# Attention feeding two mixture layers on one core: reciprocals of the row sums alone, value products in one step, the w3 @ w_out products last in the plan

## The chip, the cores and the metric

The kernel runs on one core of a Trainium2 chip. The metric is the time of one execution on the device in microseconds; lower is better. The kernel before was run three times.

## What is computed

The reference chains three blocks. Cut to what matters:

```python
# attention: batch 2, 8 heads, 576 positions, head size 64
q_rot, k_rot = rotate(q), rotate(k)
scores = q_rot @ k_rot^T / sqrt(64);  scores -= rowmax
attn = exp(scores);  attn /= rowsum(attn) + 1e-9
x = (attn @ v) laid out as 1152 x 512
# first mixture: d_model 512, d_ff 1024
h = ((x @ w1) * (x @ w2)) @ w3
x = h @ w_out
# second mixture: 8 experts, gate P balanced in 8 rounds of row and column sums
out = sum_e P[:, e] * (relu(x @ w1[e]) @ w2[e])
```

The kernel multiplies w3 @ w_out once (512 columns), so that the first mixture needs one product with the result in place of two.

## The kernel before, in words

**Attention.** A pair is two heads of one batch; there are 8 pairs (`NP`). Per pair, keys and queries are loaded, rotated (`rope_mul`, `rope_add`, `rope_hi`, `rope_lo`) and spread over partitions by DMAs from the SP queue (`spread_k`, `spread_q`). The 576 queries of each head make four tiles of 128 and one mixed tile that holds the last 64 of both heads. For every tile TensorE (PE) makes the scores (lines 340 and 363), VectorE (DVE) the negated row maximum (`row_max`, line 370), ScalarE (ACT) the exponentials with their sums in `sm` (line 374), PE transposes the exponentials (lines 388 and 391), and ACT or DVE moves them to `et` (`moved`, line 407).

Two groups of tiles (`TILES`) then have a normaliser each. `norm_sums` (line 411, ACT) adds 1e-9 to the 4 or 5 sums per partition, `norm_rows` (line 418, DVE) takes the reciprocal of the sums broadcast to 64 columns each, so of 128x256 or 128x320 elements, into `rb`; `norm_columns` (lines 424 and 427, PE) transposes that, `norm_moved` (line 432, ACT) copies it to `r`. `values` (line 440, PE) is five steps per group, two matmuls each (one per head, on the two halves of PSUM tile `x`), and `x_scale` (line 448, DVE) multiplies by `r`. `x_hi` and `x_lo` (lines 459 and 463) split the result in two parts for the fp32r products that follow. `psX` holds one PSUM tile, so the next group's first value product waits for `x_scale` of this one.

**w3 @ w_out beside it.** The weights come as 64-bit words. `wide_parts` joins their halves: ACT line 183, DVE lines 188, 191 and 196, ACT line 201 (high part), and line 204 (low part) on POOL or DVE. Eight units of w_out and sixteen of w3 are converted; there are two slots for w3. A unit of w3 gives four steps of `w34_product` (lines 231 to 233), three matmuls of 512 columns each, and frees its slot at the fourth. Two units make one of the eight row blocks, which `w34_hi` and `w34_lo` (lines 238 and 243) take out of PSUM; six blocks use `psW`, which has one tile, the seventh uses `psT`, and the eighth (`NEARLY`) comes after the plan.

**What orders it.** `Plan` (line 52) is a greedy list scheduler that runs when the kernel is built. Every step has engine costs, a rank, needs and buffers; at each moment the ready step of least rank goes out, and the resulting static order is each engine's program. The planned cost of `norm_rows` is that of a plain DVE operation of its size. Ranks of attention run with the pair's number (18 for each pair), those of `w34_product` are 87 + 4u + j for unit u and step j. Until the first `w34_product` the planned gaps on PE are filled with small matmuls (line 615).

**After the plan.** `branch` (lines 145 to 147) computes x @ w1 and x @ w2, whose weights `w12_unit` converts in the same way; the eight steps of the eighth block stand just ahead of it. `merge`, then `hidden` and `project` over the experts follow.

Of the kernel before, what the change touches and what calls it, by code (L numbers as in the profile page):

```python
# [18 lines left out]
P = 128  # L19
B, H, S, D = 2, 8, 576, 64  # L20
# [7 lines left out]
MID = NBLK // 2  # L28
SPAD = 640
NQ = NBLK // 2 + 1  # L30
MIX = NQ - 1
SF = 2 * P
HS = S // 2
G0, G1 = 256, S - 256
HD = P // 2
TILES = (0, 1), (2, 3, 4)
CN = 320, 256
# [83 lines left out]
def attention_two_moes(ctx: ExitStack, tc: tile.TileContext, rope, qk, v, mw12, mw3t, mwo, wg, ew1, ew2, out):  # L121
# [7 lines left out]
    pe, act, dve, pool, sp = nc.tensor, nc.scalar, nc.vector, nc.gpsimd, nc.sync  # L129
# [12 lines left out]
    def three(ps, terms):  # L142
# [15 lines left out]
    psS, psT, psX, psW = (  # L158
        aps.enter_context(tc.tile_pool(name=n, bufs=k, space=PSUM)) for n, k in (("psS", 2), ("psT", 2), ("psX", 1), ("psW", 1))
    )  # L160
# [63 lines left out]
    def w34_product(u, j, ps_pool, name):  # L224

        i, k = u // 2, u % 2 * 4 + j
        if k == 0:
            w34[i] = ps_pool.tile([P, DM], F32, name=name)
        (h, l, _), (oh, ol, _) = w3[u], wo[k]
        c = slice(j * P, (j + 1) * P)  # L230
        pe.matmul(w34[i], h[:, c], oh, start=(k == 0), stop=False)
        pe.matmul(w34[i], h[:, c], ol, start=False, stop=False)
        pe.matmul(w34[i], l[:, c], oh, start=False, stop=(k == KF - 1))
# [16 lines left out]
    V = [att_p.tile([P, NBLK + 1, D], F32, name=f"v{i}") for i in range(2)]  # L250
# [7 lines left out]
    raw, K, st = {}, {}, {}  # L258
# [37 lines left out]
    def spread_q(n, j, x):  # L296
# [5 lines left out]
        else:  # L302
            sp.dma_start(dst[:, : MIX * P], src[:, : MIX * P])
            sp.dma_start(dst[:, MIX * P + HD :], src[:, MIX * P :])

# [7 lines left out]
    def half(j):  # L313
        return slice(j * D, (j + 1) * D)
# [97 lines left out]

    def norm_rows(n, g):

        k = 4 + g
        sm = st["sm", n, g][:, :k]
        st["rb", n, g] = rb = att_p.tile([P, 5, D], F32, name="rb", bufs=2)
        dve.reciprocal(rb[:, :k], sm.unsqueeze(2).to_broadcast([P, k, D]))

    def norm_columns(n, g):  # L420
        rb = st["rb", n, g]
# [9 lines left out]
        ng = (G0, G1)[g]  # L431
        act.copy(r[:, :ng], st["rt", n, g].rearrange("p i q -> p (i q)")[:, :ng])

    def values(n, g, t):

        ng = (G0, G1)[g]
        if t == 0:
            st["x", n, g] = psX.tile([P, DM], F32, name="x")
        for j in range(2):
            pe.matmul(  # L440
                st["x", n, g][half(j), :ng], V[n % 2][:, 2 * t + j], st["et", n, g][:, 2 * t + j * (t < MID)],
                start=(t == 0), stop=(t == MID),
            )

    def x_scale(n, g):
        ng = (G0, G1)[g]
# [20 lines left out]
    def step(f, args, costs, rank, needs=(), takes=(), frees=(), **kw):  # L467

        many = f in (rope_mul, rope_add, rope_lo, moved, x_lo)
        plan.step((f, *args), costs, rank, lambda e: f(*args, ENG[e]) if many else f(*args), needs, takes, frees, **kw)  # L470


    act_ps, act_sb = (lambda n: 0.12 + n / 1450), (lambda n: 0.1 + n / 1190)
    on_dve, on_pool, moving = (lambda n: 0.09 + n / 945), (lambda n: 0.1 + n / 440), (lambda n: n / 250e3)
# [6 lines left out]
    for n in range(NP):  # L481
        t = n * NQ * TILE
        step(load_v, (n,), {"sp": moving(4 * P * (NBLK + 1) * D)}, t - 40.0, takes=[("v", n)])
        ready = []
        for w in (1, 0):
            pieces = (every,) if n else halves if w else (slice(0, SF), slice(SF, S))
            for c in pieces:
                a, m = (n, w, c), c.stop - c.start
                r = t - 30.0 if n else -50.0 if c.start == 0 or w else -40.0
# [8 lines left out]
                fr = [("raw", (n, w))] if n == 0 and c is pieces[-1] else []  # L498
# [6 lines left out]
            for j, x in ((j, x) for j in range(2) for x in range(2)):  # L505
# [4 lines left out]
                else:  # L510
                    needs = [((rope_hi, rope_lo)[x], n, 0, every)]
# [3 lines left out]
        for i in range(NQ):  # L515
            g, k, _ = group(i)
            r = t + i * TILE
            for j in range(2 - (i == MIX)):
# [3 lines left out]
                fr = [("kk", n), ("sq", n)] if n and i == MIX else []  # L522
                needs = ready[0] + (ready[1] if n or i * P >= SF else ready[1][:1]) + before
# [3 lines left out]
                else:  # L527
                    made = mixed_scores, n
                    if n == 0:
                        for q in range(2):  # L530
                            step(mix_first, (q,), {"act": 0.2}, r, ready[1])
                        needs = needs + [(mix_first, 0), (mix_first, 1)]
# [3 lines left out]
                fr = [("psS", (n, i, j))] + [("nm", (n, i))] * (j or i == MIX)  # L536
                step(exponentials, (n, i, j), {"act": 0.73}, r, [(row_max, n, i, j)], frees=fr)
            r += TILE
            parts = 3 - (i == MIX)
            for p in range(parts):  # L540
                needs = [(exponentials, n, i, min(p, 1) * (i < MIX))] + ([(transposes, n, i, p - 1)] if p else [(transposes, n, i - 1, 0)] if k else [])
                tk = [("psT", (n, i, p))] + ([(f"et{g}", n)] if k == p == 0 else [])
                step(transposes, (n, i, p), {"pe": 0.33}, r, needs, tk, [("e", (n, i))] if p == parts - 1 else [])
                m = 3 * (P if i < MIX else P - HD * p)
                step(moved, (n, i, p), {"act": act_ps(m), "dve": on_dve(m)}, r, [(transposes, n, i, p)], frees=[("psT", (n, i, p))])
        for g, tiles in enumerate(TILES):
            a, ng = (n, g), (G0, G1)[g]
            r = t + (tiles[-1] + 2.0) * TILE
            needs = [(exponentials, n, i, j) for i in tiles for j in range(2 - (i == MIX))]
            step(norm_sums, a, {"act": 0.2}, r, needs)  # L550
            step(norm_rows, a, {"dve": on_dve((4 + g) * D)}, r, [(norm_sums, *a)], [("rb", a)], [("sm", a)])
            step(norm_columns, a, {"pe": (0.24, 0.4)[g]}, r, [(norm_rows, *a)], [("psT", (*a, "r"))], [("rb", a)])
            step(norm_moved, a, {"act": act_ps(ng)}, r, [(norm_columns, *a)], [("r", a)], [("psT", (*a, "r"))])
            r += 3.4 * TILE
            for m in range(MID + 1):
                parts = [(i, p) for i in tiles for p in (({0, 2}, {1})[m > 2] if i < MIX else {int(m > 2)})]
                needs = [(moved, n, i, p) for i, p in parts] + [(load_v, n)]
                needs += [(values, n, g, m - 1)] if m else []
                fr = [(f"et{g}", n)] + [("v", n)] * g if m == MID else []
                step(values, (n, g, m), {"pe": ng / 600}, r, needs, [("psX", a)] if m == 0 else [], fr, paired=True)  # L560
            step(x_scale, a, {"dve": on_dve(ng)}, r, [(values, n, g, MID), (norm_moved, *a)], [("xs", a)], [("psX", a), ("r", a)])
            step(x_hi, a, {"act": act_sb(ng)}, r, [(x_scale, *a)])
            step(x_lo, a, {"pool": on_pool(ng), "dve": on_dve(ng)}, r, [(x_hi, *a)], frees=[("xs", a)], port=both)

# [20 lines left out]
    for u in range(2 * KF):  # L585
        i = u // 2
        wide_steps(w3_load, u, w3, 50.0 + 4.5 * u, [("w3", u)])
        if i == NEARLY:
            continue
        for j in range(4):  # L590
            needs = [(wo_load, u % 2 * 4 + j, 5), (w3_load, u, 5)]
            needs += [(w34_product, u, j - 1)] if j else [(w34_product, u - 1, 3)] if u else []
            bank = "psT" if i >= LATE else "psW"
            place = (psT, "t") if i >= LATE else (psW, "w34")
            plan.step(
                (w34_product, u, j), {"pe": 0.7}, 87.0 + 4 * u + j, lambda e, u=u, j=j, place=place: w34_product(u, j, *place),
                needs, [(bank, i)] if u % 2 == j == 0 else [], [("w3", u)] if j == 3 else [],
            )
        if u % 2:
            step(w34_hi, (i,), {"act": act_ps(DM)}, -200.0, [(w34_product, u, 3)])  # L600
            step(w34_lo, (i,), {"dve": on_dve(DM)}, -200.0, [(w34_hi, i)], frees=[(bank, i)])
# [159 lines left out]
    m = 14 * CN[1]  # L761
# [158 lines left out]
    for s in range(1, NSTEP):  # L920
        for c in range(2):
            for u in range(2):
# [3 lines left out]
                n = FT * (cut if u == 0 else len(done) - cut)  # L926
# [80 lines left out]
```

## Time and profile before

| | before |
|---|---|
| median of 3 runs | 1182.77 us (1182.54 to 1185.65) |
| the profiled execution, its own time | 1184.76 us |
| its span | 1183.0 us |
| PE busy | 1144.8 us (97%) |
| DVE busy | 742.6 us (63%) |
| ACT busy | 423.0 us (36%) |
| POOL busy | 200.8 us (17%) |
| granted TensorE clock, mean | 0.991 |

The attention stage is the first fifth of the span: the first matmul of `branch` starts at 249.98 us. A matmul's end in the trace is modelled, so PE time below is counted from the start of one instruction to the start of the next. The trace counts each plain f32 matmul or transpose twice, so that ten value matmuls are shown as x20.

### The profile page before, as it was taken

The page shows a single profiled execution, that of the slowest core. Times are in us where ns is not written, and L with a number is a line of the kernel's source. Part 1 is how long each engine was busy: PE and PEld are TensorE (multiplying, and loading weights), DVE is VectorE, ACT ScalarE, POOL GpSimd, SP SyncE. Part 2 cuts the span into 40 slices and gives each one's busy share as a digit, 9 for nine tenths or more (in the row PEclk, how much of TensorE's full clock was granted, in tenths as well). Part 3 has the DMA queues.
Part 4 walks back from the last instruction along what each step waited for, and adds up shares of the span by engine and source line. Part 5 has one row for each costly group of instructions (what it writes and reads, how often), then busy time and mean ns, then how long its engine had stood idle before and what let it go on. Part 6 is the DMA issues. An engine that isn't in the chain of part 4 may idle for free.

```text
span 1183.0 us, 17650 instructions
## 1 busy us (share of the span) xinstructions
PE 1144.8 (97%) x7058; PEld 1006.9 (85%) x7058; DVE 742.6 (63%) x1325; ACT 423.0 (36%) x900; POOL 200.8 (17%) x202
## 2 busy tenths in 40 slices
PE   9997998999999999999999999999999999999998
PEld 7675676678999988899898898989988989889887
DVE  7898787767533476656556566656565566665643
ACT  5675565534332333322323233222232323232311
POOL 3443462132100000211101111011021110101100
PEclk9998999999999999999999999999999999999999
DMA  6764565233100011111102111111021111110102
GB/s 209 211 220 147 173 164 139 89 96 119 54 19 19 5 51 36 54 54 36 55 18 72 37 36 55 52 38 54 19 72 37 36 54 41 50 53 20 36 9 71
DMA packets 29153, 83.07 MB, mean 70 GB/s; under 512 B 4880, under 2 KB 6416, under 8 KB 29072
## 3 DMA queue, kind: packets, MB, share of 16 engines
q1 hardware_dynamic: 28528, 81.36, 21.9%
q8 instruction: 55, 0.90, 0.3%
q10 hardware_dynamic: 544, 0.59, 0.2%
q14 instruction: 26, 0.21, 0.1%
HBM read 67.19 MB, written 2.36 MB: 59 GB/s over the span
## 4 chain that ended last, share of the span: by engine, by line
PE 83%; DVE 9%; DMA 3%; issue 2%; ACT 2%; POOL 1%; SPq 0%; ACTq 0%; DVEq 0%; POOLq 0%
PE z L838 11%; PE z L837 11%; PE z L839 11%; PE T L796 4%; PE T L797 4%; PE T L798 4%; PE Q L798 3%; PE Q L796 3%; PE Q L797 3%; PE A L798 3%; PE A L797 3%; PE A L796 3%; PE u L145 3%; PE u L147 3%; PE u L146 3%; PE x L440 2%
## 5 line engine op out<-in xcount | busy, mean ns | idle before, releaser
L839 PE MATMUL z<-w,h 128*128 128x512 f32 x576 | 226.3, 393 | 0.0
L846 DVE SCALAR_TENSOR_TENSOR acc<-z,pr,acc 128x512 f32<-128x512 f32 x135 | 101.0, 748 | 56.6 <-PE z L839 56.5
L839 PEld LDWEIGHTS z<-w,h 128*128 128x128 f32 x576 | 108.0, 187 | 25.3
L838 PE MATMUL z<-w,y 128*128 128x512 f32 x320 | 126.4, 395 | 0.0
L837 PE MATMUL z<-w,y 128*128 128x512 f32 x320 | 126.3, 395 | 0.0
L716 POOL TENSOR_TENSOR sums<-wide 128x256 f32<-128x256 f32 x28 | 22.8, 816 | 575.2 <-DMA wide<-in_ew_dram 340.2
L838 PE MATMUL z<-w,h 128*128 128x512 f32 x256 | 101.6, 397 | 0.0
L837 PE MATMUL z<-w,h 128*128 128x512 f32 x256 | 100.8, 394 | 0.0
L139 ACT CAST w<-wide 128x768 fp32r<-128x768 f32 (+1 forms) x64 | 60.3, 943 | 93.4 <-PE z L838 65.0
L140 DVE TENSOR_TENSOR w<-wide,w 128x768 fp32r<-128x768 f32 (+1 forms) x64 | 69.7, 1089 | 26.5 <-PE T L798 14.8
L802 ACT ACTIVATE y<-tmp 128x320 fp32r<-128x320 f32 x96 | 45.2, 470 | 113.8 <-DVE tmp L818 62.2
L802 ACT ACTIVATE h<-tmp 128x256 fp32r<-128x256 f32 x96 | 40.0, 416 | 127.5 <-DVE tmp L818 120.8
L145 PE MATMUL u<-x,w 128*128 128x320 f32 (+1 forms) x256 | 76.4, 298 | 3.8 <-DVE gf L658 2.6
L147 PE MATMUL u<-x,w 128*128 128x320 f32 (+1 forms) x256 | 75.7, 296 | 0.0
L146 PE MATMUL u<-x,w 128*128 128x320 f32 (+1 forms) x256 | 75.4, 295 | 0.0
L838 PEld LDWEIGHTS z<-w,y 128*128 128x128 f32 x320 | 60.7, 190 | 5.7
L837 PEld LDWEIGHTS z<-w,y 128*128 128x128 f32 x320 | 60.2, 188 | 6.0
L803 DVE SCALAR_TENSOR_TENSOR h<-tmp,y 128x320 fp32r<-128x320 f32 x96 | 47.5, 494 | 26.0 <-ACT y L802 25.8
L374 ACT ACTIVATE e<-s,nm 128x576 f32<-128x576 f32 x72 | 53.3, 742 | 25.8 <-DVE nm L370 25.4
L796 PE MATMUL T<-x,w 128*128 128x320 f32 x192 | 60.0, 312 | 0.1
L370 DVE TENSOR_REDUCE nm<-s 128x1 f32<-128x576 f32 x72 | 52.3, 745 | 11.8 <-PE s L340 9.6
L440 PE MATMUL x<-et,v 128*64 128x256 f32 (+1 forms) x320 | 50.9, 438 | 8.7 <-DVE xs L448 8.7
(224 smaller groups left out, 3042.6 us busy)
## 6 DMA issues: line engine op xcount, KB each, us to landing
wide<-in_ew_dram SPq DMA_DIRECT2D x64, 512.0 KB, 3.5
wide<-in_mw3t_dram SPq DMA_DIRECT2D x16, 512.0 KB, 4.2
wide<-in_mw_dram SPq DMA_DIRECT2D x16, 512.0 KB, 3.5
raw<-in_qk_dram SPq DMA_DIRECT2D x14, 576.0 KB, 5.1
kk<-raw SPq DMA_DIRECT2D x56, 144.0 KB, 2.5
wide<-in_mwo_dram SPq DMA_DIRECT2D x8, 512.0 KB, 6.5
v<-in_v_dram SPq DMA_DIRECT2D x8, 320.0 KB, 4.0
out_dram<-acc SPq DMA_DIRECT2D x8, 256.0 KB, 2.0
```

The source lines that it names most:

```text
L145: pe.matmul(ps, wh, xh, start=(i == 0), stop=False)
L146: pe.matmul(ps, wh, xl, start=False, stop=False)
L147: pe.matmul(ps, wl, xh, start=False, stop=(i == n - 1))
L440: pe.matmul(st["x", n, g][half(j), :ng], V[n % 2][:, 2 * t + j], st["et", n, g][:, 2 * t + j * (t < MID)], start=(t == 0), stop=(t == MID),)
L796: pe.matmul(ps, h[:, ws], x[0], start=(first and k == 0), stop=False, **kw)
L797: pe.matmul(ps, h[:, ws], x[1], start=False, stop=False, **kw)
L798: pe.matmul(ps, l[:, ws], x[0], start=False, stop=(k == 1), **kw)
L802: act.activation(h, src, AF.Relu)
L837: pe.matmul(ps, hh[:, f, ts], wh, start=(f == 0), stop=False)
L838: pe.matmul(ps, hh[:, f, ts], wl, start=False, stop=False)
L839: pe.matmul(ps, hl[:, f, ts], wh, start=False, stop=(f == FT - 1))
L846: dve.scalar_tensor_tensor(out=acc[t], in0=ps, scalar=p, in1=acc[t], op0=ALU.mult, op1=ALU.add)
```

## The change

Three edits. `norm_rows` becomes the reciprocal of the 4 or 5 sums in place, and a new step `norm_spread` on ACT copies it, broadcast, into `rb`. `values` does all five blocks of a group in one step (`VPARTS`), so its ten matmuls stand together and need all moved tiles of the group. The rank of `w34_product` becomes 1000 + 4u + j, so that every ready step of attention goes ahead of it.

```diff
--- before.py
+++ after.py
@@ -32,6 +32,7 @@
 SF = 2 * P
 HS = S // 2
 G0, G1 = 256, S - 256
+VPARTS = (0, 1, 2, 3, 4),
 HD = P // 2
 TILES = (0, 1), (2, 3, 4)
 CN = 320, 256
@@ -412,10 +413,14 @@
 
     def norm_rows(n, g):
 
+        sm = st["sm", n, g][:, : 4 + g]
+        dve.reciprocal(sm, sm)
+
+    def norm_spread(n, g):
+
         k = 4 + g
-        sm = st["sm", n, g][:, :k]
         st["rb", n, g] = rb = att_p.tile([P, 5, D], F32, name="rb", bufs=2)
-        dve.reciprocal(rb[:, :k], sm.unsqueeze(2).to_broadcast([P, k, D]))
+        act.copy(rb[:, :k], st["sm", n, g][:, :k].unsqueeze(2).to_broadcast([P, k, D]))
 
     def norm_columns(n, g):
         rb = st["rb", n, g]
@@ -431,16 +436,17 @@
         ng = (G0, G1)[g]
         act.copy(r[:, :ng], st["rt", n, g].rearrange("p i q -> p (i q)")[:, :ng])
 
-    def values(n, g, t):
+    def values(n, g, part):
 
         ng = (G0, G1)[g]
-        if t == 0:
+        if part == 0:
             st["x", n, g] = psX.tile([P, DM], F32, name="x")
-        for j in range(2):
-            pe.matmul(
-                st["x", n, g][half(j), :ng], V[n % 2][:, 2 * t + j], st["et", n, g][:, 2 * t + j * (t < MID)],
-                start=(t == 0), stop=(t == MID),
-            )
+        for t in VPARTS[part]:
+            for j in range(2):
+                pe.matmul(
+                    st["x", n, g][half(j), :ng], V[n % 2][:, 2 * t + j], st["et", n, g][:, 2 * t + j * (t < MID)],
+                    start=(t == 0), stop=(t == MID),
+                )
 
     def x_scale(n, g):
         ng = (G0, G1)[g]
@@ -548,17 +554,19 @@
             r = t + (tiles[-1] + 2.0) * TILE
             needs = [(exponentials, n, i, j) for i in tiles for j in range(2 - (i == MIX))]
             step(norm_sums, a, {"act": 0.2}, r, needs)
-            step(norm_rows, a, {"dve": on_dve((4 + g) * D)}, r, [(norm_sums, *a)], [("rb", a)], [("sm", a)])
-            step(norm_columns, a, {"pe": (0.24, 0.4)[g]}, r, [(norm_rows, *a)], [("psT", (*a, "r"))], [("rb", a)])
+            step(norm_rows, a, {"dve": 0.12}, r, [(norm_sums, *a)])
+            step(norm_spread, a, {"act": act_sb((4 + g) * D)}, r, [(norm_rows, *a)], [("rb", a)], [("sm", a)])
+            step(norm_columns, a, {"pe": (0.24, 0.4)[g]}, r, [(norm_spread, *a)], [("psT", (*a, "r"))], [("rb", a)])
             step(norm_moved, a, {"act": act_ps(ng)}, r, [(norm_columns, *a)], [("r", a)], [("psT", (*a, "r"))])
             r += 3.4 * TILE
-            for m in range(MID + 1):
-                parts = [(i, p) for i in tiles for p in (({0, 2}, {1})[m > 2] if i < MIX else {int(m > 2)})]
-                needs = [(moved, n, i, p) for i, p in parts] + [(load_v, n)]
+            for m, blocks in enumerate(VPARTS):
+                parts = {(i, p) for i in tiles for t in blocks for p in (({0, 2}, {1})[t > 2] if i < MIX else {int(t > 2)})}
+                needs = [(moved, n, i, p) for i, p in sorted(parts)] + [(load_v, n)]
                 needs += [(values, n, g, m - 1)] if m else []
-                fr = [(f"et{g}", n)] + [("v", n)] * g if m == MID else []
-                step(values, (n, g, m), {"pe": ng / 600}, r, needs, [("psX", a)] if m == 0 else [], fr, paired=True)
-            step(x_scale, a, {"dve": on_dve(ng)}, r, [(values, n, g, MID), (norm_moved, *a)], [("xs", a)], [("psX", a), ("r", a)])
+                last = m == len(VPARTS) - 1
+                fr = [(f"et{g}", n)] + [("v", n)] * g if last else []
+                step(values, (n, g, m), {"pe": len(blocks) * ng / 600}, r, needs, [("psX", a)] if m == 0 else [], fr, paired=True)
+            step(x_scale, a, {"dve": on_dve(ng)}, r, [(values, n, g, len(VPARTS) - 1), (norm_moved, *a)], [("xs", a)], [("psX", a), ("r", a)])
             step(x_hi, a, {"act": act_sb(ng)}, r, [(x_scale, *a)])
             step(x_lo, a, {"pool": on_pool(ng), "dve": on_dve(ng)}, r, [(x_hi, *a)], frees=[("xs", a)], port=both)
 
@@ -593,7 +601,7 @@
             bank = "psT" if i >= LATE else "psW"
             place = (psT, "t") if i >= LATE else (psW, "w34")
             plan.step(
-                (w34_product, u, j), {"pe": 0.7}, 87.0 + 4 * u + j, lambda e, u=u, j=j, place=place: w34_product(u, j, *place),
+                (w34_product, u, j), {"pe": 0.7}, 1000.0 + 4 * u + j, lambda e, u=u, j=j, place=place: w34_product(u, j, *place),
                 needs, [(bank, i)] if u % 2 == j == 0 else [], [("w3", u)] if j == 3 else [],
             )
         if u % 2:
```

The plan turns these into other orders on all engines. On DVE, around the fifth of the 16 reciprocals, before (`nm` is the row maximum, `et` a moved transpose, `cvu` a weight conversion, `xs` the scaled values):

```order
L370 TENSOR_REDUCE nm<-s 128x1 x2
L407 COPY et_731<-t 128x3x128
L418 RECIPROCAL rb<-sm 128x256
L370 TENSOR_REDUCE nm<-s 128x1 x4
L407 COPY et_837<-t 128x3x128
```

and now:

```order
L454 TENSOR_TENSOR xs<-x,r 128x320
L371 TENSOR_REDUCE nm<-s 128x1
L417 RECIPROCAL sm<-sm 128x4
L408 COPY et_754<-t 128x3x128
L371 TENSOR_REDUCE nm<-s 128x1
```

The reciprocal has 4 columns in place of 256; the copy to `rb` now stands in ACT's program, 16 times. On all of DVE the new order also takes six more `et` copies of 3x128 and two more of 3x64 in exchange for one of 6x64 and gives four `x_lo` and one `rope_mul` to POOL.

On PE, the second group of the first pair (`rb` the normaliser's transposes, `x` the value products, `s` scores, `t` transposes), before:

```order
L427 MATMUL t<-ident,rb 64x64 x2
L440 MATMUL x<-et_296,v_94 64x320 x2
L388 MATMUL t<-ident,e 128x128 x3
L340 MATMUL s<-kk,sq_93 128x288 x4
L440 MATMUL x<-et_296,v_94 64x320 x2
L388 MATMUL t<-ident,e 128x128 x6
L340 MATMUL s<-kk,sq_93 128x288 x4
```

and now:

```order
L432 MATMUL t<-ident,rb 64x64 x2
L446 MATMUL x<-et_313,v_94 64x320 x10
L389 MATMUL t<-ident,e 128x128 x6
L341 MATMUL s<-kk,sq_93 128x288 x8
L389 MATMUL t<-ident,e 128x128 x3
L623 MATMUL w_104<-ident 128x128 x9
```

The value products of the 16 groups stand in 43 runs before and in 16 now.

On PE, the end of attention (line 145 or 146 is the first matmul of `branch`; `w_2186` and `w_2372` are two row blocks of w3 @ w_out), before:

```order
L424 MATMUL t<-ident,rb 128x128 x2
L427 MATMUL t<-ident,rb 64x64 x2
L440 MATMUL x<-et_2393,v_95 64x320 x10
L231 MATMUL u<-y 128x512
L232 MATMUL u<-y 128x512
L233 MATMUL u<-y 128x512
...
L145 MATMUL u<-x,w_2498 128x320
```

and now:

```order
L432 MATMUL t<-ident,rb 64x64 x2
L232 MATMUL w_2186<-y 128x512
L233 MATMUL w_2186<-y 128x512
L234 MATMUL w_2186<-y 128x512
L446 MATMUL x<-et_2226,v_95 64x320 x10
L232 MATMUL w_2186<-y 128x512
L233 MATMUL w_2186<-y 128x512
L234 MATMUL w_2186<-y 128x512
L232 MATMUL w_2372<-y 128x512
...
L146 MATMUL u<-x,w_2521 128x320
```

Behind the last value products stand 8 steps of w3 @ w_out before (24 matmuls, all of the eighth block) and 33 now (99 matmuls). On DVE, 4 conversions (line 188, now 189) stand between the last `xs` and the first product of `branch` before, 10 now.

## Rows read from the trace of the kernel before

**Rows 1.** The page: busy time of each engine, share of the span, instructions.
```profile
PE 1144.8 (97%) x7058; PEld 1006.9 (85%) x7058; DVE 742.6 (63%) x1325; ACT 423.0 (36%) x900; POOL 200.8 (17%) x202
```

**Rows 2.** Busy time by stretch: PE, PEld, DVE, ACT, POOL, granted clock, DMA share, GB/s.
```profile
0.00:250.00 250.00, 221.60 (x1442) 165.59 (x1443) 197.19 (x276) 144.43 (x343) 93.97 (x67) 0.96 0.54 160
60.00:90.00 30.00, 27.14 (x200) 20.51 (x199) 27.14 (x34) 20.29 (x49) 14.92 (x8) 1.00 0.65 211
300.00:350.00 50.00, 50.00 (x377) 50.00 (x376) 22.71 (x47) 16.91 (x38) 2.74 (x2) 1.00 0.13 43
```

**Rows 3.** DVE groups by shape, 0 to 244 us: busy, mean ns; then idle before them.
```profile
L196 DVE SCALAR_TENSOR_TENSOR cvu<-cvy,cvu 128x512 int32<-128x512 int32 x26 | 24.5, 943 | 1.0
L407 DVE COPY et<-t 128x384 f32<-128x384 f32 x42 | 22.8, 550 | 11.0 <-PE t L388 10.9
L191 DVE SCALAR_TENSOR_TENSOR cvu<-wide,cvu 128x512 int32<-128x512 int32 x26 | 21.4, 823 | 0.8
L418 DVE RECIPROCAL rb<-sm 128x320 f32<-128x320 f32 x8 | 17.2, 2147 | 2.5 <-ACT sm L411 2.5
L418 DVE RECIPROCAL rb<-sm 128x256 f32<-128x256 f32 x8 | 14.0, 1747 | 0.7 <-ACT sm L411 0.7
L188 DVE TENSOR_SCALAR cvu<-wide 128x512 int32<-128x512 int32 x26 | 13.9, 534 | 2.1 <-POOL y L204 2.0
L463 DVE TENSOR_TENSOR x<-xs,x 128x320 fp32r<-128x320 f32 x4 | 2.0, 490 | 1.9 <-ACT x L459 1.9
```

**Rows 4.** PE's waits, 0 to 350 us: total, times, longest.
```profile
PE t L424 <- DVE rb L418: 5.3, 7, 1.3
```

**Rows 5.** A reciprocal of 9 columns (min/median/max ns); ACT's copy of 320 columns (busy, mean ns).
```profile
L892 DVE RECIPROCAL rs<-rs x8: 204/212/217, 422.7 to 453.7; 128x9 f32<-128x9 f32 x8
...
L459 ACT CAST x<-xs 128x320 fp32r<-128x320 f32 x7 | 3.2, 456 | 4.6 <-DVE xs L448 4.6
```

**Rows 6.** POOL and DVE in order of time; then line 191 alone (min/median/max ns).
```profile
118.12 3.13 POOL L272 TENSOR_TENSOR raw<-raw,tab 128x1152 f32<-128x1152 f32 x1 [2.70 <-DMA raw<-in_qk_dram]
119.33 2.21 DVE L188 TENSOR_SCALAR cvu<-wide 128x512 int32<-128x512 int32 x1
...
L191 DVE SCALAR_TENSOR_TENSOR cvu<-wide,cvu x27: 682/693/3026, 13.9 to 249.1; 128x512 int32<-128x512 int32 x27
```

**Rows 7.** PE in order of time: start, us; value products split and together.
```profile
103.74 0.76 PE L440 MATMUL x<-et,v 128*64 128x320 f32 x4
104.43 0.87 PE L388 MATMUL t<-ident,e 128*128 128x128 f32 x6
...
223.30 2.91 PE L440 MATMUL x<-et,v 128*64 128x320 f32 x20
```

**Rows 8.** PE in order of time: steps of w3 @ w_out, and a change of the PSUM tile.
```profile
109.78 0.39 PE L231 MATMUL w<-y 128*128 128x512 f32 x1
...
110.47 0.39 PE L231 MATMUL w<-y 128*128 128x512 f32 x1
...
111.62 0.40 PE L233 MATMUL w<-y 128*128 128x512 f32 x1
...
113.42 0.50 PE L231 MATMUL w<-y 128*128 128x512 f32 x1 [0.87 <-DVE keep L243]
```

**Rows 9.** PE in order of time: mixed scores of pairs 2 and 7, the end of attention.
```profile
72.98 1.42 PE L363 MATMUL s<-kk,sq 128*128 128x288 f32 x10
...
231.63 1.40 PE L363 MATMUL s<-kk,sq 128*128 128x288 f32 x10
...
239.28 4.42 PE L440 MATMUL x<-et,v 128*64 128x320 f32 x20
...
249.98 0.31 PE L145 MATMUL u<-x,w 128*128 128x320 f32 x1
```

**Rows 10.** The two parts of a converted weight (min/median/max ns).
```profile
L204 POOL TENSOR_TENSOR y<-cvu,y x15: 1273/1283/1307, 25.9 to 228.3; 128x512 fp32r<-128x512 f32 x15
...
L201 ACT CAST y<-cvu x24: 609/620/639, 17.7 to 227.6; 128x512 fp32r<-128x512 f32 x24
```

## The prediction

> **What bounds the kernel now.** I read the page first: PE is busy 97% of the span, but that share is an average over unlike stages [rows 1]. The busy times by stretch separate them. From 300 us on PE is busy all the time at full clock while DVE has half its time free [rows 2]; nothing that shortens DVE or reorders attention reaches that part. In the first 250 us, the attention stage, DVE is busy 197.2 us, a share of 0.789, and in a stretch well inside it 27.1 of 30 us, as full as PE's 27.1 [rows 2]. PE's own figure there is padded with filler matmuls and modelled ends. So I take the attention stage as paced mainly by DVE and by the hand-overs that queue behind it, and look for what the three edits do to the moment at which `branch` starts, now 249.98 us [rows 9].
>
> The groups of DVE instructions show where its time goes. The 16 reciprocals of broadcast sums take 17.2 + 14.0 = 31.2 us, 1.75 or 2.15 us each [rows 3]. The order was planned with each of them at the cost of an ordinary operation of that size; an ordinary one of 320 columns takes 0.49 us on DVE [rows 3]. Each one therefore runs over by some 1.5 us, and every later step of DVE's fixed order slips behind it. PE's direct wait for the result, 5.3 us in all [rows 4], is only the visible part; the row maxima and moves queued behind the reciprocal are late too.
>
> **The reciprocals.** A reciprocal of 9 columns takes 0.212 us [rows 5]; one of 4 or 5 columns can't cost more, and I take 0.21. DVE gets 31.2 - 16 x 0.21 = 27.8 us back. ACT gets 16 copies of 256 or 320 columns. Its copy of 320 columns takes 0.456 us [rows 5], so at most 16 x 0.456 = 7.3 us more for ACT, which is busy 144.4 of 250 us [rows 2]: it has the room. In the chain from sums to normaliser a 1.95 us step (the mean of the two) becomes 0.21 + 0.46 and one hand-over, over a microsecond shorter, so the added step doesn't make the value products late.
>
> **Work that changes engine.** DVE takes six more moves of 0.55 us and gives up four low parts of at most 0.49 us [rows 3]: +3.3 and -2.0 us. The rest of the exchange, two short moves more and one rotation multiply fewer, I set at nothing, which is on the cautious side. DVE's net is 27.8 - 1.3 = 26.5 us less, 170.7 in place of 197.2 us. POOL gains five operations and was busy 94.0 of 250 us [rows 2], so they are covered.
>
> **The value products.** Four records of a split run take 0.69 us from start to start (103.74 to 104.43), so 20 would take 3.45 us; together 20 take 2.91 us [rows 7]. The order has 43 runs before and 16 after; 27 breaks at about (3.45 - 2.91) / 4 = 0.13 us are 3.6 us of PE. The price of the edit: all moves of a group must be there before its first product. That is hidden as long as PE has scores, transposes or w3 @ w_out steps to go on with, which the new order puts there.
>
> **The products of w3 @ w_out.** A step of three matmuls takes 0.69 us (109.78 to 110.47) [rows 8]. Behind the last value products stand 8 steps now (5.5 us) and 33 afterwards: 22.8 us. With the steps back to back, a change of PSUM tile is bare: from the last matmul of one block at 111.62 to the first of the next at 113.42, less 0.23 us for the matmul itself, is 1.6 us [rows 8], with four score matmuls in it. Two such changes fall in the tail, 3.2 us, so it takes 26 us. This isn't all loss: 25 steps, 17.3 us, are work that no longer stands in front of attention steps. Before, they did: from the mixed scores of pair 2 (72.98) to those of pair 7 (231.63) five pairs took 158.7 us [rows 9].
>
> **The sum.** If DVE keeps its present share of 0.789, 170.7 us of work reach to 216.4 us. Counted the other way, along the order: the first 73.0 us lose 6 reciprocals at 1.74 us, 10.4; the 158.7 us of the five pairs lose 10 reciprocals (17.4), 25 steps (17.3) and some 2.5 us of value runs, leaving 121.5; from the last mixed scores to the last value product it is now 243.7 - 231.6 = 12.1 us, and I keep 10; then the tail of 26. That gives 62.6 + 121.5 + 10 + 26 = 220 us. I take 217 to 218, nearer to the first because the second credits nothing for late work that catches up, and 1 us more for `branch`, which finds its weights converted later (10 conversions stand on DVE between the last scaled values and its first product, 4 before). The stage is then 32 us shorter. The rest of the kernel is PE-bound and unchanged. The profiled execution took 1184.76 us, 2.0 us above the median of 1182.77; the same 32 us off the median give 1151 us. Bounds of this case: DVE at 0.75 of its time gives 170.7 / 0.75 = 228 us and a time of 1162; at 0.83 it gives 206 us and 1140.
>
> **A rule that speaks against it.** While POOL multiplies for 3.13 us from 118.12 us, a DVE conversion that started at 119.33 lasts 2.21 us and ends within 0.3 us of POOL's end [rows 6]. Undisturbed, line 191 takes 0.693 us (its median), and lines 191 and 196, 52 operations of one form, have means of 0.823 and 0.943 us [rows 3, 6]: 26 x 0.13 + 26 x 0.25 = 9.9 us lost. The Trainium skill (SBUF — State Buffer, section "SBUF: two separate sides") says that DVE and GpSimd share a port pair as an exclusive lock, held for a whole instruction. The row agrees with it. By that rule the same POOL work in a shorter stage meets DVE more often: 9.9 x 250 / 217 = 11.4 us, so about 1.5 us less gain than the sum.
>
> **The rivals.**
> *Freed DVE time goes to waiting for POOL.* The reciprocals were 31 us in which POOL could run without stopping a conversion. If conversions move into POOL's time until the 9.9 us lost double, and line 188 loses its share, some 14 us of the gain go: 1165 us. For it: rows 6. Against: POOL is busy only 94 of 250 us.
> *More than the sum.* With DVE as full as at 60 to 90 us, 0.905 [rows 2], 170.7 us reach to 189 us, the tail then becomes the bound, and `branch` starts near 200: 1133 us. For it: the plan's costs now fit DVE. Against: the tail of 26 us needs an attention that ends at 174.
> *Slower: the tail waits for w3.* Only two slots hold converted units, and with all steps last the remaining units are converted while PE consumes them. If the slots don't overlap, each unit costs its high part on ACT (0.62), its low part on POOL (1.28) [rows 10] and four steps (2.77): 4.7 us. The 33 steps are 8.25 units, 38.5 us. DVE's own 10 conversions of 0.53 + 0.82 + 0.94 = 2.3 us [rows 3] make 23 us and alone don't reach that. If also nothing but the removed steps shortens attention (73.0 + 141.4 + 12.1 = 226.5 us), `branch` starts at 265: 1198 us. It decides from an attention that ends later than 211 us. Against: two slots can alternate, and DVE's relief would have to vanish.
> *It does next to nothing.* Another loop, the loads and spreads of the next pair, could hold the pairs at their pace: 1181 us. Against: PE's waits name DVE and not DMA there [rows 4].
>
> **How the numbers follow.** Chances: the forecast 0.62 (1151, its own range 1140 to 1162), POOL waits 0.17 (1165), more than the sum 0.10 (1133), slower tail 0.07 (1198), nothing 0.04. The range from 1135 to 1170 holds the first two whole and the near part of the third. About 0.3%, 3.5 us, is what a measurement can tell from no change: faster by more 0.89, within it 0.04, slower by more 0.07.
>
> **What would show it.** Right: the 16 reciprocals at 0.2 us each; ACT's spread copies under 0.5 us; DVE near 171 us before `branch`; the first matmul of `branch` near 217 us; the 33 steps in 24 to 30 us; the span after that as long as now, 933 us. Wrong: waits of PE for line 204 or 243 inside the tail, a tail over 35 us; conversions on lines 188 to 196 with higher means than now; PE idle ahead of value products for a late move; a granted clock in the stage below the present 0.96 [rows 2].

## The result, and the profile after

| | time, us | runs | ratio to before, 95% |
|---|---|---|---|
| before | 1182.72 | 4 | |
| after | 1165.82 (1165.04 to 1167.42) | 4 | 0.9853 [0.9834, 0.9872] |

The change makes the kernel 1.5% faster, some 17 us. The forecast was 1151 us: the direction is right and the time lies in the range, but of the 32 us that were forecast about half is missing. The execution that was profiled took 1167.42 us, with a span of 1165.1 us.

Three lines answer to those of before. The page's engines, against [rows 1]:

```profile
PE 1138.6 (98%) x7072; PEld 1010.2 (87%) x7072; DVE 717.8 (62%) x1327; ACT 425.5 (37%) x909; POOL 207.3 (18%) x207
```

DVE is busy 24.8 us less in the whole kernel. The stretches, in the columns of [rows 2], with the attention stage now cut at 233 us because `branch` starts there:

```profile
0.00:233.00 233.00, 215.05 (x1454) 168.67 (x1455) 171.45 (x281) 147.07 (x353) 99.83 (x72) 0.98 0.59 173
60.00:90.00 30.00, 27.47 (x190) 20.37 (x187) 20.69 (x32) 18.90 (x47) 22.15 (x14) 0.89 0.62 179
300.00:350.00 50.00, 50.00 (x372) 50.00 (x371) 19.44 (x38) 15.99 (x35) 0.00 (x0) 1.00 0.10 32
```

DVE's work in the stage came out as forecast, 171.45 us (170.7 was the sum). Its share did not stay: 171.45 / 233 = 0.736, and 20.7 of 30 us in the inner stretch, which had been 27.1. So DVE had less to do and then waited more. The granted clock of the stage is 0.98, 0.96 before. An estimate from these rows, were PE the limit throughout: 0.04 x 250 = 10 us and 0.02 x 233 = 4.7 us go to the clock, so up to 5 us of the gain may be clock. It is not what separates the runs below: e3 has 0.99 up to `branch` and gains nothing. PE stays full from 300 us on, as before.

DVE's groups by shape in the first 228 us, against [rows 3], and then, of another view, ACT's new copies (min/median/max ns, first and last start):

```profile
L192 DVE SCALAR_TENSOR_TENSOR cvu<-wide,cvu 128x512 int32<-128x512 int32 x25 | 22.6, 904 | 0.7
L197 DVE SCALAR_TENSOR_TENSOR cvu<-cvy,cvu 128x512 int32<-128x512 int32 x25 | 22.4, 895 | 0.9
...
L417 DVE RECIPROCAL sm<-sm 128x5 f32<-128x5 f32 x8 | 1.5, 187 | 2.6 <-ACT sm L412 2.5
L417 DVE RECIPROCAL sm<-sm 128x4 f32<-128x4 f32 x8 | 1.4, 173 | 5.3 <-ACT sm L412 5.3
```

```profile
L423 ACT COPY rb<-sm x16: 389/436/472, 20.9 to 196.9; 128x256 f32<-128x256 f32 x8, 128x320 f32<-128x320 f32 x8
```

The 16 reciprocals take 2.9 us in place of 31.2, ACT's copies 0.39 to 0.47 us each. The two conversion lines have means of 0.904 us (192, which was 191: 0.823) and 0.895 us (197, which was 196: 0.943) [rows 3].

PE in order of time (start, us): the mixed scores of pairs 2 and 7, the last value products, the first matmul of `branch`. They answer to [rows 9].

```profile
72.91 1.41 PE L364 MATMUL s<-kk,sq 128*128 128x288 f32 x10
...
193.22 1.32 PE L364 MATMUL s<-kk,sq 128*128 128x288 f32 x10
...
200.53 2.91 PE L446 MATMUL x<-et,v 128*64 128x320 f32 x20
...
233.28 0.31 PE L146 MATMUL u<-x,w 128*128 128x320 f32 x1
```

Pair 2 gets there at the same moment as before (72.98). The five pairs after it take 120.3 us in place of 158.7, and attention ends at 203.4 us in place of 243.7, 40.3 us earlier. Then the tail takes 29.8 us where 6.3 us stood (243.7 to 249.98), 23.6 us more. The difference, 16.7 us, is the gain up to `branch`. What follows `branch` takes 931.8 us, 933.0 before.

### The profile page after: what moved, and what is told of

Same layout as the page of the kernel before. It is cut to its first block, busy times and chain, and to the rows that moved or that the text cites. A ratio compares the mean times of both kernels' runs of the same rounds, so it can differ in the third digit from the quotient of the medians.

```text
span 1165.1 us, 17715 instructions
## 1 busy us (share of the span) xinstructions
PE 1138.6 (98%) x7072; PEld 1010.2 (87%) x7072; DVE 717.8 (62%) x1327; ACT 425.5 (37%) x909; POOL 207.3 (18%) x207
## 4 chain that ended last, share of the span: by engine, by line
PE 86%; DVE 6%; DMA 3%; ACT 1%; issue 1%; POOL 1%; SPq 1%; DVEq 0%; POOLq 0%; ACTq 0%
PE z L846 12%; PE z L845 11%; PE z L847 11%; PE T L804 4%; PE T L805 4%; PE T L806 4%; PE u L146 3%; PE u L148 3%; PE u L147 3%; PE Q L806 3%; PE Q L804 3%; PE Q L805 3%; PE A L806 3%; PE A L805 3%; PE A L804 3%; PE x L446 2%
## 5 line engine op out<-in xcount | busy, mean ns | idle before, releaser
L804 PE MATMUL T<-x,w 128*128 128x320 f32 x192 | 59.9, 312 | 0.0
L805 PE MATMUL T<-x,w 128*128 128x320 f32 x192 | 59.2, 309 | 0.0
L806 PE MATMUL T<-x,w 128*128 128x320 f32 x192 | 59.0, 308 | 0.0
```

The source lines that it names most:

```text
L804: pe.matmul(ps, h[:, ws], x[0], start=(first and k == 0), stop=False, **kw)
L805: pe.matmul(ps, h[:, ws], x[1], start=False, stop=False, **kw)
L806: pe.matmul(ps, l[:, ws], x[0], start=False, stop=(k == 1), **kw)
```

## Experiments

The change has three parts: the reciprocals of the sums alone with ACT's copies (here R), the value products of a group in one step (V), and the late rank of the w3 @ w_out products (K). The first five runs take them singly and in two of the three pairs; V with K, without R, was not run. Each ratio is against runs of the kernel before on the same chip.

**e1_recip_only**: the changed kernel with V and K undone.

```diff
-VPARTS = (0, 1, 2, 3, 4),
+VPARTS = (0,), (1,), (2,), (3,), (4,)
...
-                (w34_product, u, j), {"pe": 0.7}, 1000.0 + 4 * u + j, ...
+                (w34_product, u, j), {"pe": 0.7}, 87.0 + 4 * u + j, ...
```

> Reciprocals of the sums alone and the copy on ACT, but value products in five steps per group and w3 @ w_out at its old ranks (87). Theory R (the gain is DVE time given back): nearly all of the 17 us, 1165 to 1171. Theory W (the gain is that w3 @ w_out no longer stands in front of attention): under 5 us, 1178 to 1183. In both, the mixed scores of pair 2 stay near 73 us, since the loads and rotations of the next pair hold the first pairs.

Measured: 1181.37 us, 0.9976 [0.9956, 0.9996]. The part that I had made nearly the whole gain gives 2.8 us alone by the ratio (0.5 to 5.2 by its interval), and 0.8 us by the medians. DVE was relieved as planned, in the first 250 us (columns as above):

```profile
0.00:250.00 250.00, 225.39 (x1480) 170.42 (x1481) 174.50 (x279) 150.32 (x358) 101.56 (x73) 0.97 0.58 162
```

It is busy 174.5 us where it was 197.2 [rows 2], and `branch` still starts at 246.98. The freed time became idle time. So DVE's load was not what paced this order. One expectation missed: the mixed scores of pair 2 come at 79.28 us and not near 73.

**e2_recip_values** (R and V, second hunk of e1 alone):

```diff
-                (w34_product, u, j), {"pe": 0.7}, 1000.0 + 4 * u + j, ...
+                (w34_product, u, j), {"pe": 0.7}, 87.0 + 4 * u + j, ...
```

> As the change, with the ranks of w3 @ w_out left at 87. Theory R: within 3 us of the change, 1163 to 1169, and 3 to 4 us below the reciprocals alone if joining the value products is worth its 27 breaks at 0.13 us. Theory W: 1175 to 1182.

Measured: 1164.56 us, 0.984 [0.9778, 0.9903], which can't be told from the whole change. Its four runs lie far apart, 1159.9 to 1175.8 us. The mixed scores of pairs 2 and 7 and the first matmul of `branch`:

```profile
71.39 1.41 PE L364 MATMUL s<-kk,sq 128*128 128x288 f32 x10
...
215.46 1.40 PE L364 MATMUL s<-kk,sq 128*128 128x288 f32 x10
...
231.85 0.31 PE L146 MATMUL u<-x,w 128*128 128x320 f32 x1
```

**e3_recip_rank** (R and K, first hunk of e1 alone):

```diff
-VPARTS = (0, 1, 2, 3, 4),
+VPARTS = (0,), (1,), (2,), (3,), (4,)
```

> As the change, with the value products in five steps per group. If joining them is worth 27 breaks at 0.13 us of PE, 1168 to 1170; if PE is not what binds while attention runs, 1165 to 1167; if joining them makes them late, below 1164.

Measured: 1181.24 us, 0.9998 [0.9969, 1.0027], above everything that was expected. With the value products split, attention ends early here too (last one at 207.7 us), but `branch` starts at 245.07: only 20 of the 64 steps of w3 @ w_out had run when the value products ended.

**e4_rank_only** (K in the kernel before):

```diff
-                (w34_product, u, j), {"pe": 0.7}, 87.0 + 4 * u + j, ...
+                (w34_product, u, j), {"pe": 0.7}, 1000.0 + 4 * u + j, ...
```

> The kernel before with w3 @ w_out last in rank, nothing else. Theory R: DVE is as late as before and the tail is longer, 1178 to 1190. Theory W: most of the gain, 1167 to 1174.

Measured: 1178.5 us, 0.9959 [0.9936, 0.9982].

**e5_values_only** (V; R and K undone):

```diff
-        sm = st["sm", n, g][:, : 4 + g]
-        dve.reciprocal(sm, sm)
...
-        act.copy(rb[:, :k], st["sm", n, g][:, :k].unsqueeze(2).to_broadcast([P, k, D]))
+        dve.reciprocal(rb[:, :k], sm.unsqueeze(2).to_broadcast([P, k, D]))
...
-            step(norm_rows, a, {"dve": 0.12}, r, [(norm_sums, *a)])
-            step(norm_spread, a, {"act": act_sb((4 + g) * D)}, r, [(norm_rows, *a)], [("rb", a)], [("sm", a)])
...
+            step(norm_rows, a, {"dve": on_dve((4 + g) * D)}, r, [(norm_sums, *a)], [("rb", a)], [("sm", a)])
...
-                (w34_product, u, j), {"pe": 0.7}, 1000.0 + 4 * u + j, ...
+                (w34_product, u, j), {"pe": 0.7}, 87.0 + 4 * u + j, ...
```

> The kernel before with the value products joined, nothing else: reciprocals of 1.75 to 2.15 us stay, w3 @ w_out stays at rank 87. Theory V (the joining alone carries the gain, by the order that it makes): 1163 to 1169. Theory RV (joining and short reciprocals are worth something only together, since a late DVE then holds the joined products): 1176 to 1186. The sum of my prediction (3.6 us for the joining): 1179.

Measured: 1176.14 us, 0.9951 [0.9931, 0.9972].

The five together: R alone is worth 0.2%, V alone 0.5%, K alone 0.4%, and R with V 1.6%. On top of V, R is worth (0.9951 - 0.984) x 1183 = 13 us, with some 8 us of uncertainty, nearly all of it from e2; on split value products it is worth 3 us, and beside K it loses 4.6 (0.9959 to 0.9998). K adds nothing measurable to R and V. **In these runs DVE's relief pays where the value products of a group are one step, and hardly where they are split at their late rank.**

Two groups of split value products in e1, in PE's order of time (start, us; the trace counts 20 matmul records to a group):

```profile
106.07 0.65 PE L446 MATMUL x<-et,v 128*64 128x256 f32 x4
...
107.12 0.65 PE L446 MATMUL x<-et,v 128*64 128x256 f32 x4
...
110.58 1.52 PE L446 MATMUL x<-et,v 128*64 128x256 f32 x12
...
118.36 0.76 PE L446 MATMUL x<-et,v 128*64 128x320 f32 x4
...
119.91 0.71 PE L446 MATMUL x<-et,v 128*64 128x320 f32 x4
...
122.75 1.83 PE L446 MATMUL x<-et,v 128*64 128x320 f32 x12
```

and two groups in the changed kernel:

```profile
101.62 2.38 PE L446 MATMUL x<-et,v 128*64 128x256 f32 x20
...
112.60 2.91 PE L446 MATMUL x<-et,v 128*64 128x320 f32 x20
```

From 106.07 to 112.10 a group of e1 takes 6.0 us, from 118.36 to 124.58 the next 6.2 us; joined they take 2.4 and 2.9. Over all 16 groups the mean from the first product's start to the last one's end is 6.8 us before, 6.4 in e1 and 6.2 in e3, and 2.7 in e2, e5 and after. The value steps carry a late rank, so at each of four boundaries the plan may put something else first, while the moved scores `et` and the PSUM tile of the group stay taken.

To test that it is the rank that makes splitting dear, two runs give the value steps the rank of the normaliser's steps. The edit also takes along the steps behind them, `x_scale`, `x_hi` and `x_lo`, whose rank is the same variable `r`.

**e8_split_urgent** (the changed kernel, split again, but with the early rank) and **e9_joined_urgent** (the early rank alone, the second hunk):

```diff
-VPARTS = (0, 1, 2, 3, 4),
+VPARTS = (0,), (1,), (2,), (3,), (4,)
...
-            r += 3.4 * TILE
+            r += 0.0 * TILE
```

> The change with value products in five steps per group, but their rank 12.2 lower, so that they go out as soon as they are ready. Theory T (split products trickle behind scores and so hold et and the PSUM tile for the next group; joining cures that): 1164 to 1171, most of the loss of the split kernel comes back. Theory S (splitting costs PE by itself, through changes of weight width and small gaps): as the split kernel with both other edits, 1178 to 1184.

> The change with the joined value products' rank 12.2 lower as well. Theory T (what counts is how long a group holds et and the PSUM tile once it could go): joining has cured that already, within 4 us of the change, 1162 to 1170. If the rank still delays joined groups: 1155 to 1161.

Measured: e8 1168.78 us, 0.988 [0.985, 0.9911]; e9 1167.59 us, 0.9863 [0.9817, 0.9909]. e8 differs from e3 by these ranks alone, and 1.2% of time. Its groups span 3.7 us in the mean, and its time is 3 us above that of the change, with intervals that overlap. On joined steps the same rank does nothing measurable (e9 against after). So splitting costs mostly through the late ranks, little by the breaks themselves. Whether it is the rank of the products or that of `x_scale`, which empties the PSUM tile, these two runs don't separate.

**e6_wide_recip_pairs_0_2** and **e7_wide_recip_pairs_3_7** put DVE's time back into the change: an extra reciprocal of the broadcast sums into a scratch tile that nothing reads, in pairs 0 to 2 or in pairs 3 to 7 (`n > 2`). The planned cost is not touched, and PE, ACT and SP run their instructions in the same order as in the changed kernel.

```diff
         sm = st["sm", n, g][:, : 4 + g]
+        if n < 3:
+            wide = att_p.tile([P, 5, 56], F32, name="burn")
+            dve.reciprocal(wide[:, : 4 + g], sm.unsqueeze(2).to_broadcast([P, 4 + g, 56]))
         dve.reciprocal(sm, sm)
```

> The change in its own order, with a broadcast reciprocal of 4 or 5 x 56 columns (1.55 to 1.9 us on DVE) put back beside each of the first 6 short ones. If loads and rotations hold the first three pairs: within 3 us of the change, 1163 to 1168. If DVE holds them: 6 x 1.7 = 10 us more, 1176.

> The same for the last 10 short reciprocals. If DVE's relief is worth its time there, as the prediction had it: 10 x 1.7 = 17 us more, 1178 to 1184. If the gain is the order alone: within 4 us of the change, 1163 to 1170.

Measured: e6 1167.87 us, 0.9873 [0.9847, 0.99]; e7 1178.19 us, 0.9957 [0.9939, 0.9974]. What was put back, in e6 and then e7 (busy us, mean ns):

```profile
L419 DVE RECIPROCAL burn<-sm 128x280 f32<-128x280 f32 x3 | 5.7, 1896 | 0.1
...
L419 DVE RECIPROCAL burn<-sm 128x224 f32<-128x224 f32 x3 | 4.6, 1547 | 1.8 <-ACT sm L412 1.8
```

```profile
L419 DVE RECIPROCAL burn<-sm 128x280 f32<-128x280 f32 x5 | 9.5, 1903 | 2.3 <-ACT sm L412 2.3
...
L419 DVE RECIPROCAL burn<-sm 128x224 f32<-128x224 f32 x5 | 7.7, 1547 | 1.9 <-ACT sm L412 1.9
```

10.3 us in the first three pairs cost (0.9873 - 0.9853) x 1183 = 2.4 us, within the uncertainty of nothing; 17.2 us in the last five cost (0.9957 - 0.9853) x 1183 = 12.3 us. In this order an added microsecond on DVE costs about 0.7 us from pair 3 on, and little before. Not all of that need be DVE's queue: the added reciprocal stands ahead of the short one, so it delays the normaliser too. In e7 PE waits for `rb` (up to 246 us; us in total, times, longest), and in the changed kernel nowhere in the stage:

```profile
PE t L432 <- ACT rb L426: 5.3, 4, 1.6
...
PE t L392 <- ACT rb L426: 1.6, 1, 1.6
```

**e11_longer_rotation** asks what paces the first pairs. From pair 1 on it lengthens each rotation of q and k by one copy, into a half of the tile that the next step (`rope_hi`) overwrites.

```diff
+        if n:
+            eng.tensor_copy(t[:, 1, c], t[:, 0, c])
```

> The change with one more POOL copy of 128x576 (about 1.4 us) behind each rotation, so some 2.8 us more per pair in the loop of loads, rotations and spreads; it computes nothing new. If that loop holds the first pairs: the mixed scores of pair 2 come 3 to 6 us later than 72.9 us and the time is 1169 to 1182. If the loop has slack: mixed scores of pair 2 within 1 us, time within 2 us of the change.

Measured: 1169.46 us, 0.988 [0.9839, 0.992], some 3 us slower than the change, with intervals that overlap. A copy takes 0.66 us (median, on POOL), half of what I had expected. SP's first loads for pairs 3 and 4 (start, us), after, then e11, then e6:

```profile
53.66 0.54 SPq L265 DMA_DIRECT2D raw<-in_qk_dram  x1
...
71.82 0.34 SPq L265 DMA_DIRECT2D raw<-in_qk_dram  x1
```

```profile
54.63 0.54 SPq L265 DMA_DIRECT2D raw<-in_qk_dram  x1
...
73.28 0.34 SPq L265 DMA_DIRECT2D raw<-in_qk_dram  x1
```

```profile
54.79 0.54 SPq L265 DMA_DIRECT2D raw<-in_qk_dram  x1
...
73.44 0.34 SPq L265 DMA_DIRECT2D raw<-in_qk_dram  x1
```

The mixed scores of pair 2 come at 74.54 us in e11, 1.6 us later than in the change. But e6, whose rotations are those of the change, has its loads as late and these scores at 75.17, and e7, which changes nothing ahead of them, has them at 73.38. Nor does the delay of the loads grow by two copies a pair, as it would if the loop set the pace: it is 1.0 and then 1.5 us. So what paces the first pairs is not shown.

**e10_late4** and **e12_late4_spread_act** try to better the change. The tail of the change shows PE waiting for PSUM tiles to be emptied (us in total, times, longest; 203 to 234 us):

```profile
PE w L232 <- DVE keep L244: 2.9, 2, 1.5
PE u L232 <- DVE keep L244: 2.0, 1, 2.0
```

e10 lets the blocks of w3 @ w_out use the attention's transpose tiles from block 4 on in place of block 6. e12 does the same and moves the spreads of q from SP's queue to ACT's.

```diff
-LATE = 6
+LATE = 4
```

and for e12 also

```diff
-            sp.dma_start(dst[:, :S], src)
+            act.dma_start(dst[:, :S], src)
...
-                    step(spread_q, (n, j, x), {"sp": moving(4 * D * S)}, t - 30.0, needs, frees=[("raw", (n, 0))])
+                    step(spread_q, (n, j, x), {"act": 0.1 if j == 0 else 0.2}, t - 30.0, needs, frees=[("raw", (n, 0))])
```

> The change with blocks 4 and 5 of w3 @ w_out in the two-tile PSUM pool of the transposes in place of the one-tile pool, so that two changes of block in the tail have a second tile to go to. If PE's 2.9 us of waits for line 244 in the tail are real cost: 1162 to 1163.5. If the conversion of w3 then becomes the wait: 1165 to 1166.5. If the blocks take tiles from the transposes: above 1167.

> The change with blocks 4 and 5 in the two-tile pool (as in the run before) and the six spreads of each pair's queries issued from ACT's queue in place of SP's, so that SP's loop of a pair loses about 4.5 us of issuing. If the loop of loads, rotations and spreads holds the first pairs and SP's issuing is a part of it: mixed scores of pair 2 before 71 us and 1154 to 1160. If the loop's transfers and rotations hold it, not the issuing: 1160 to 1163. If the issuing on ACT delays exponentials: above 1163.

Measured: e10 1161.5 us (1161.25 to 1161.97), 0.9816 [0.9778, 0.9853], a little under what was expected. This is the fastest version by its median, 4.3 us under the change, though the intervals touch; its PE waits in the tail (200 to 228 us) are

```profile
PE u L232 <- DVE keep L244: 2.0, 1, 2.0
```

alone, and its tail takes 26.4 us (200.85 to 227.27), 3.4 us less. Another 2.6 us come from an attention that ends earlier, so not all of the difference is the PSUM tiles'.

e12 missed: 1182.86 us, 1.0003 [0.9977, 1.003]. The last expectation allowed a loss if ACT's issuing delays exponentials; that this is the cause is not shown. The whole gain is gone although value products are joined (2.6 us a group) and reciprocals short. The mixed scores of pair 2 come at 81.89 us, those of pair 7 at 222.38, `branch` at 242.32, only 6.3 us after the last value product: the plan had placed nearly all of w3 @ w_out ahead of it in spite of K. The stretch up to 73 us in e10, then in e12:

```profile
0.00:73.00 73.00, 67.95 (x517) 56.71 (x518) 52.18 (x89) 47.31 (x113) 37.92 (x33) 1.00 0.68 208
```

```profile
0.00:73.00 73.00, 64.18 (x479) 53.81 (x479) 46.35 (x79) 42.13 (x101) 36.01 (x31) 1.00 0.70 205
```

Every compute engine has done less in e12 by then. The plan put the whole stage into another order, and which of its moves costs the time is open. It shows that joined values are not enough for the gain: the planner's order can lose as much by another route.

## Why the prediction was right, and where it failed

- **What bounds the stage: a busy share did not show it.** I read DVE's share of 0.789, and 27.1 of 30 us inside, as the pace. e1 takes 22.7 us of that work away and gains 2.8 us. A busy engine that is relieved and then idles was following something else; e1 has its own order, so of the order before this is argued, not shown. PE's direct waits were the better hint, and [rows 4] is not their longest. That is for the PSUM tile of the value products (0 to 350 us, before):

```profile
PE x L440 <- DVE xs L448: 8.7, 2, 5.9
```

The first of the two, before (start, us):

```profile
86.37 3.03 DVE L191 SCALAR_TENSOR_TENSOR cvu<-wide,cvu 128x512 int32<-128x512 int32 x1
...
90.61 3.06 POOL L272 TENSOR_TENSOR raw<-raw,tab 128x1152 f32<-128x1152 f32 x1
...
91.12 3.09 DVE L196 SCALAR_TENSOR_TENSOR cvu<-cvy,cvu 128x512 int32<-128x512 int32 x1
...
95.27 2.40 PE L440 MATMUL x<-et,v 128*64 128x320 f32 x8 [5.87 <-DVE xs L448]
```

The scaling that empties the tile stood on DVE behind conversions of 3.03 and 3.09 us, against a median of 0.69 [rows 6], while POOL multiplied. So DVE's time counted there by its place in the order, not by its sum. The change has no such wait, but its end is not the whole gain: e1, which has none either, gains 2.8 us. In the change's own order, from pair 3 on, added DVE work does cost time (e7).

- **The sum over DVE's constant share: failed.** 170.7 / 0.789 = 216.4 us needed a share that stays. The work was right (171.45), the share fell to 0.736.
- **The additive sum, 62.6 + 121.5 + 10 + 26 = 220 us, against 72.9 + 120.3 + 10.2 + 29.8, in the trace 233.3 us.** The first term is the step that failed: 10.4 us credited for six reciprocals up to the mixed scores of pair 2, and nothing came. It was miscounted, since only five of them start ahead of those scores (the sixth starts at 81.39 us), and it was mis-sized: e6 puts five, 8.4 us, back there, the scores come 2.3 us later, and by `branch` nothing of it is left (232.57 us against 233.28).
- **The second term came out by luck.** I had 17.4 us for reciprocals and 2.5 for the values, and 17.3 for steps moved out of the way. In e2, where the steps are not moved, the five pairs take 215.46 - 71.39 = 144.1 us: reciprocals and values are worth 14.6 us there, 5.3 less than the 19.9 that I had. With the steps moved the five pairs take 120.3 us: that is 23.8 us for the steps, 6.5 more than the 17.3. The tail, 6.2 us in e2 and 29.8 now, gives 23.6 us of them back, so moving the steps gains nothing measurable. The third term came out.
- **The fourth term, the tail, was too short by 3.8 us.** I had counted two changes of PSUM tile for 3.2 us, and the trace has three waits for them, 2.9 + 2.0 = 4.9 us. Behind the third the clock fell, in the columns of [rows 2]:

```profile
226.10:229.50 3.40, 3.40 (x8) 2.72 (x9) 2.70 (x3) 1.29 (x3) 1.76 (x2) 0.50 0.38 135
```

At 0.50 a step takes 1.28 us (227.55 to 228.83) where I had 0.69; by an estimate from this row it is 1.7 us more.

- **The value products: mis-sized, by missing the mechanism.** I priced 27 breaks at 0.13 us, 3.6 us. That is what a break costs PE, not what giving way costs the stage. From e1 to e2, which differ in this edit alone, the ratio falls by 1.4%, 16 us.
- **The choice of 217 to 218 us** lay nearer to the first sum, since the second credits no late work that catches up. The second was the nearer to 233. That the time still lies in the range is in part luck, since the cause that I gave for the gain did not hold.
- **The rivals.** *POOL waits* named 1165 us, which is what came, and its mechanism did not: by the median of 0.693 us [rows 6] the two conversion lines lose 25 x (0.904 + 0.895 - 1.386) = 10.3 us, where 9.9 was the loss before. The rule of the Trainium skill (SBUF — State Buffer, section "SBUF: two separate sides") would, by my estimate, have made it 11.4 us; the loss stayed about the same, so by this count it took at most some 0.4 us of the gain that is missing. *More than the sum* needed DVE fuller; it got emptier. *Slower tail* did not come: PE's waits in the tail, the two rows ahead of e10's diff, name no converted weight. *Another loop holds the pairs* was given 0.04 because PE's waits named no DMA; for pairs 0 to 2 the runs leave it open (e6, e11), for the later ones e7 speaks against it.
- **The signs of being wrong.** PE's waits for line 243, now 244, did come inside the tail, 4.9 us; the sum had 3.2 of them. The mean of one conversion line rose and that of the other fell. The granted clock of the stage did not fall.
- **Details that held:** DVE near 171 us, reciprocals near 0.2 us, ACT's copies under 0.5 us, 931.8 us after `branch` (933 forecast).

What stays open: why reciprocals and joined values are worth more together. One figure of the traces goes with the time: how long a group keeps the one PSUM tile of `psX`, from the start of its first value product to the end of `x_scale`, in the mean of the 16 groups.

| | before | e4 | e1 | e3 | e5 | e12 | e8 | e2 | e11 | e9 | change | e10 |
|---|---|---|---|---|---|---|---|---|---|---|---|---|
| us | 10.2 | 9.2 | 9.0 | 8.8 | 8.3 | 8.0 | 6.3 | 6.1 | 5.5 | 5.3 | 5.2 | 5.1 |
| ratio | 1 | 0.9959 | 0.9976 | 0.9998 | 0.9951 | 1.0003 | 0.988 | 0.984 | 0.988 | 0.9863 | 0.9853 | 0.9816 |

All runs up to e12 gain 0.5% or less, those from e8 on 1.2% or more. e6 and e7, which add work to DVE in the order of the change, both have 5.3 us, so e7 loses its time by another path. The moved scores `et` do not sort the runs: from the first move to the last value product they are held for 18.5 us in e2 and 18.2 in e3. The figure goes with the time and is no proof of a cause: no run changed the tile alone, and a second `et` was not tried. Each edit of cost or rank also reorders the whole stage, so a single cell of the first five runs contains some luck of the order; e6, e7 and e11, which keep the order, do not.

## What to carry to other kernels

An engine's high busy share does not show that it sets the pace: take work from it, or put work back, without touching the order, stretch by stretch, before a gain is credited. In a planned order, ask of each low-ranked step what it holds while it gives way, and make it one step or rank it early if others need that. Follow the longest wait of the busiest engine back to what stood ahead in the queue it waited for. When work is moved to the end to clear the way, count its waits for tiles as well as its matmuls.

## What the runs showed of the hardware

A reciprocal of broadcast sums costs by its columns: 1.55, 1.75, 1.90 and 2.15 us for 224, 256, 280 and 320 columns, 6.7 to 6.9 ns a column, while 4 and 5 columns take 0.173 and 0.187 us. A subtraction of 320 columns takes 0.49 us [rows 3], under a quarter of it.

On POOL a copy takes about half of what an addition of the same shape takes: the two lines of e11, over the whole span (min/median/max ns, first and last start):

```profile
L277 POOL TENSOR_TENSOR raw<-raw x13: 1403/1435/1860, 17.5 to 166.3; 128x576 f32<-128x576 f32 x13
...
L279 POOL COPY raw<-raw x13: 662/665/1013, 19.3 to 167.8; 128x576 f32<-128x576 f32 x13
```

A short wait for a spread of q was followed by half speed. In the changed kernel, PE's order of time:

```profile
77.86 0.77 PE L341 MATMUL s<-kk,sq 128*128 128x288 f32 x4 [1.94 <-DMA sq<-raw]
...
82.94 4.50 PE L446 MATMUL x<-et,v 128*64 128x320 f32 x20
```

and two stretches behind the wait, in the columns of [rows 2]:

```profile
79.00:82.90 3.90, 3.88 (x19) 2.77 (x19) 3.16 (x4) 2.98 (x7) 3.11 (x4) 0.55 0.47 163
82.90:87.40 4.50, 4.50 (x22) 1.94 (x21) 1.95 (x2) 1.39 (x4) 4.42 (x3) 0.64 0.49 154
```

After PE had idled for 1.94 us the granted clock was 0.55 and then 0.64, that is for the most part the lower level of 1.2 GHz in place of 2.4, and 20 value products took 4.50 us where they take 2.91 at 200.53. In e10 PE idled 2.04 us until 77.90, its clock fell too, but was back at the higher level for the same products, at 82.64:

```profile
77.90:81.40 3.50, 3.50 (x17) 3.01 (x17) 1.40 (x2) 1.08 (x3) 3.50 (x3) 0.51 0.66 206
...
82.64:85.48 2.84, 2.84 (x21) 1.35 (x20) 2.48 (x3) 1.95 (x5) 2.37 (x2) 1.00 0.56 141
```

From the end of the wait to the first step behind the products the same steps took 9.5 us in the change (77.86 to 87.37) and 7.6 in e10 (77.90 to 85.48): a wait of nearly the same length cost 1.9 us more in one run than in the other.
